# A fused attention and two-MLP kernel: its opening stage in a hand-written order

## The chip, the cores and the metric

One Trainium2 chip, of which the kernel uses one core. The metric is device time in microseconds for one execution; lower is better. Three runs of the kernel before took 1207.8, 1211.51 and 1207.32 us.

## The reference

The inputs are q, k, v (8 batches, 8 heads, 576 rows, 64 columns) and phi (the same with 32 columns), all float32; the weights W1 (512 x 2048) and W2 (2048 x 512) of the first MLP, and those of the second one, are float64 in memory.

```python
a = exp(phi - max(phi, axis=2)); a = a / (sum(a, axis=2) + 1e-9)
k_m = einsum('bhsm,bhsd->bhmd', a, k); v_m = einsum('bhsm,bhsd->bhmd', a, v)
attn = softmax(0.125 * q @ k_m.T)
x = attn @ v_m                                   # heads side by side: 8 x 576 x 512
xn = (x - mean(x)) / sqrt(var(x) + 1e-6) * g_ln
x = x + relu(xn @ W1) @ W2                       # first MLP
h = gelu(x @ w_in); u, v = halves of h           # second MLP
x = x + (u * (w_sg @ norm(v) + b_sg)) @ w_out
```

## The kernel before

The program has two phases. Phase 1 computes attention and the first MLP for the eight batches in turn, phase 2 the second MLP. All matrix products are made in float32 by splitting an operand into a high and a low part (suffixes h and l) that TensorE multiplies in separate passes.

In phase 1 attention is not multiplied out. For each batch `prep_max`, `prep_exp`, `prep_sum`, `prep_kv` and `prep_norm` make the 32 memory rows per head (`kvn`) from phi, k and v; `prep_T` turns them (`kvT`); `prep_vb` lays the value part out as `VBh`/`VBl`. For each group of query tiles (128 rows each, with a short tile of 64 at the end of a batch) `t_q` turns the tile through TensorE (`ptq`, copied to `qT`), `t_scores` makes the scores (`sc`), turns them on VectorE (`z`) and takes the exponential, `t_norm` divides by the sum, `t_attn` turns back and splits into `aTh` and `aTl`. `t_x` multiplies with VB to get x itself (`px`).

W1 is treated in four column blocks of 512 (fb = 0 to 3), each made of four row blocks (j = 0 to 3) of 128 x 512. `load_w1` brings the float64 words (`raw`), 512 KB for each row block in two loads. `to_f32` makes float32 of them: a ScalarE pass over the high words (L112), a VectorE pass over the low words (L113, one input), and a VectorE pass that joins both (L114, two inputs). `scale_w1` multiplies with the gain g1c on ScalarE, to `wc` (L498). `center_w1` subtracts the mean over rows: four matmuls with a constant column (`cm`, L504) add up the row blocks and spread the mean, VectorE subtracts (L506). `make_vw` multiplies the centered block with the memory's value part (`pvw`, L544), so that the hidden layer of the MLP follows directly from the attention weights, and `evict_vw` splits the result (`vw`, L550 on ScalarE, L551 on VectorE). `m1` multiplies `aT` with `vw` to the hidden tile `ph` (L592), `relu` evicts it (`hh` on ScalarE L578, `hl` on VectorE L579; `cr` is the part carried to the next batch), `m2` multiplies with W2 to `py` (L622 to L624). W2 comes in 16 chunks of 128 rows: `load_w2`, then `split_w2` with the same conversion, a cast on ScalarE (`whl`, L126) and a remainder on POOL (L127).

Batch 0 goes through the column blocks with both of its row groups (256 and 320 rows) inside, so each column block has 4 x 2 hidden tiles and needs four chunks of W2.

What sets the order: every step is put on a list with a time by `at_time`, the list is sorted, and `run_until` traces the steps. Then a scheduler orders the instructions of each engine by its own timeline; it may move what was traced later ahead of what was traced earlier. Loads are all issued by the SP queue through `load`, at most eight outstanding. `issue_after` holds an instruction behind another one.

The opening, up to time -0.4 on the list, makes batch 0's memory rows, all five query tiles of its attention (two groups of two and the short one), the first W1 block, and the first chunks of W2. Of the calls that place W1's blocks:

```python
at_time((-26.5, -26.2, -2.5, 2.0)[fb], load_w1, fb)
at_time((-16.5, -5.0, 3.0, 7.5)[fb], scale_w1, fb)
at_time((-16.4, -0.3, 4.6, 9.1)[fb], center_w1, fb)
```

Of the kernel before, what the change touches and what calls it, by code (L numbers as in the profile page):

```python
# [9 lines left out]
F32 = mybir.dt.float32  # L10
# [5 lines left out]
ALU = mybir.AluOpType  # L16
# [8 lines left out]
ORDER = mybir.DependencyInfo(mybir.DependencyClass.Sync, mybir.DependencyReason.DATA)  # L25


@with_exitstack
def fused_kernel(ctx: ExitStack, tc: tile.TileContext, q, k, v, phi, g1, w1, w2, w_in, g2, w_sg, b_sg, w_out, out):
    nc = tc.nc  # L30
    PE, V, A, G = nc.tensor, nc.vector, nc.scalar, nc.gpsimd

    B, H, S, D = q.shape
    NM = phi.shape[3]
    DM = H * D
    FF = w1.shape[1]
    P = 128
    NF = FF // P
    NFB = FF // DM
    KC = DM // P  # L40
# [26 lines left out]
    mean = mcol.to_broadcast([P, P])  # L67
    mhalf = const.tile([P, 3], F32, name="mhalf")
    G.memset(mhalf, -0.5)
    g1c = const.tile([P, KC], F32, name="g1c")  # L70
    g2c = const.tile([P, KC], F32, name="g2c")
# [10 lines left out]
        return t[:, 0, :], t[:, 1, :]  # L82

    def load(out_ap, in_ap):
        return nc.sync.dma_start(out=out_ap, in_=in_ap)  # L85

    def rsqrt_of(tmp, x, on_v):

# [54 lines left out]
    def phase1():  # L143
# [24 lines left out]
        def ps_of(b, shape, name):  # L168
            return ps_0(shape, name) if b == 0 else ps_a.tile(shape, F32, tag="a", name=name)
# [307 lines left out]
        W2, WC, VW, raws = {}, {}, {}, {}  # L477

        def wc_tiles():
            return [tail.tile([P, 2, DM], F32, tag="wc", name="wc", bufs=4) for _ in range(2)]  # L480

        def load_w1(fb):

            raws[fb] = []
            for j in range(KC):
                t = wpool.tile([P, DM], I64, tag="w", name="raw1")
                for g in range(2):
                    r0 = g * 4 * D + j * D
                    load(t[64 * g:64 * g + 64, :], w1[r0:r0 + D, fb * DM:(fb + 1) * DM])
                raws[fb].append(t)  # L490

        def scale_w1(fb):

            WC[fb] = ws = wc_tiles()
            for j, raw in enumerate(raws.pop(fb)):
                d = ws[j // 2][:, j % 2, :]
                w = to_f32(raw, [st.get("hl", tiles[TB - 1]["tr"])] if fb else None)
                A.activation(d, w, AF.Copy, scale=g1c[:, j:j + 1])  # L498

        def center_w1(fb):  # L500
            ws = WC[fb]
            cm = ps_of(fb, [P, DM], "cm")
# [131 lines left out]
        def at_time(time, fn, *a):  # L634
            ev.append((time, seq[0], fn, a))
            seq[0] += 1
# [9 lines left out]
        for b in range(B):  # L646
            pair, odd = divmod(b, 2)
# [10 lines left out]
            for n, gs in enumerate([[0], [1]] if b == 0 else [[0, 1]]):  # L658
                at_time(pb - (4.3 if b == 3 else 5) * f, load_phi, b, gs)
                at_time(pb + 0.2 * n, prep_max, b, gs)  # L660
                at_time(pb + 0.1 + 0.2 * n if b == 0 else pb + f, prep_exp, b, gs)
            at_time(pb + (1.6 if b else 6) * f, prep_sum, b)
            kv_at = (4.0, 6.7) if b == 0 else (5.2, 7.4) if odd and b > 1 else (4.4, 8.4)
            at_time(pb - 2 if b == 0 else pb + 0.6 * f, load_rem, b)
            if b > 1:
                at_time(pb + 7.0 * f, prep_kv, b, [0, 1])
            for g in range(2):
                if b <= 1:
                    at_time(pb + kv_at[g] * f, prep_kv, b, [g])
                for part in range(2):  # L670
                    n = 2 * g + part
                    if b == 0:
                        kv_from = pb - 4 + n
                    elif b == 1:
                        kv_from = pb + (0.5 * part if g == 0 else kv_at[0] + 0.1 + 0.01 * part) * f
                    else:
                        kv_from = pb + (0.5 + 1.2 * n) * f
                    at_time(kv_from, load_kv, b, g, part)
            if b == 0:
                for g in range(2):  # L680
                    at_time(pb + 9.3 * f, prep_norm, b, g)
            at_time(first - 0.6, prep_T, b)
            at_time(first + (0.8 if b == 1 else 3), prep_vb, b)
# [50 lines left out]
        def run_until(time):  # L734
            while ev and ev[0][0] <= time:
                _, _, fn, a = ev.pop(0)
                fn(*a)

        for fb in range(NFB):
            at_time((-26.5, -26.2, -2.5, 2.0)[fb], load_w1, fb)  # L740
            at_time((-16.5, -5.0, 3.0, 7.5)[fb], scale_w1, fb)
            at_time((-16.4, -0.3, 4.6, 9.1)[fb], center_w1, fb)
            at_time((-15, 1.3, 5.8, 10.3)[fb], make_vw, 0, [fb])
            at_time((-15, 1.3, 5.8, 10.3)[fb], evict_vw, 0, fb)
            at_time((1.4, 3.0, 7.4, 12.0)[fb], store_w1, fb)
        for c in range(NF):
            split_at = 4.5 * (c // 4) + 0.5625 * (c % 4) - 0.6 if c > 3 else 0.9 * c - 4
            at_time(split_at - 5 if c > 3 else -12.7 if c == 3 else 0.2 * c - 26.4, load_w2, c)
# [21 lines left out]
        for n in range(len(steps) + LAG):  # L770
# [4 lines left out]
            if n >= LAG:  # L775
                _, j, c = steps[n - LAG]
# [310 lines left out]
        es_left.close()  # L1087
        es_right.close()

    for g in range(2):  # L1090
        load(g1c[64 * g:64 * g + 64, :], g1[g * 4 * D:(g + 1) * 4 * D].rearrange("(c p) -> p c", p=D))
    load(g2c, g2.rearrange("(c p) -> p c", p=P))
    phase1()
    phase2()

# [29 lines left out]
```

## Time and profile before

| | |
|---|---|
| median of 3 runs | 1207.8 us (1207.32 to 1211.51) |
| span of the profiled execution | 1206.0 us, from its first to its last instruction; no separate time of that execution is given, the runs' median is 1.8 us above its span |
| TensorE matmuls busy | 1167.4 us, 97% |
| VectorE, ScalarE, POOL busy | 689.7, 467.1, 400.7 us |
| granted TensorE clock, mean | 0.990 |
| moved by DMA | 124.15 MB, mean 103 GB/s |

How to read it: busy time is the time in which an engine executes instructions; matmuls are pipelined, so their durations overlap and the distance of two starts is their price. The granted clock is 1.00 at 2.4 GHz and 0.50 at 1.2 GHz. In a timeline a row may stand for several instructions (x4); its second number is then the time from the first one's start to the last one's end. The bracket at a row's end is the idle time of the engine before it and what ended that. In a row of the DMA queue (SPq) the time is that of issuing, not of the transfer.

### The profile page before, as it was taken

What the parts mean: (1) busy time and instruction counts of PE and PEld (TensorE: products, weight loads), DVE (VectorE), ACT (ScalarE), POOL (GpSimd) and SP (SyncE); (2) the same over time, 40 slices, a digit from 0 to 9 for tenths busy, and PEclk for the clock granted to TensorE, in tenths of its full rate; (3) what the DMA queues carried; (4) which work ended last, traced back from release to release, by engine and by line L of the source; (5) the groups of instructions that cost most, each with busy time, mean ns of one, the idle gap of its engine ahead of it and who ended that gap; (6) DMA issues with size and microseconds to landing.
All of it is one profiled execution on the core that took longest, in us unless ns stands there. A gap on an engine that the chain in (4) does not pass through costs nothing.

```text
span 1206.0 us, 20725 instructions
## 1 busy us (share of the span) xinstructions
PE 1167.4 (97%) x7711; PEld 991.3 (82%) x7711; DVE 689.7 (57%) x1669; ACT 467.1 (39%) x1071; POOL 400.7 (33%) x622
## 2 busy tenths in 40 slices
PE   4699999999999999999999999999999999999998
PEld 2377678888788888788888888889989988998997
DVE  2887665755645545644645445568576477447532
ACT  3575333332432322332323445445444354344430
POOL 2133212211201211201211112456666475566641
PEclk9699999999999999999999999999999999999999
DMA  8996744373341443331410343122240042022201
GB/s 205 284 287 177 219 106 125 79 205 66 109 117 31 129 137 66 97 107 23 128 36 27 106 118 115 35 82 88 77 143 18 19 142 77 1 81 86 79 18 70
DMA packets 199141, 124.15 MB, mean 103 GB/s; under 512 B 93312, under 2 KB 174336, under 8 KB 199040
## 3 DMA queue, kind: packets, MB, share of 16 engines
q1 hardware_dynamic: 199040, 122.82, 36.4%
q8 instruction: 61, 1.00, 0.3%
q14 instruction: 40, 0.33, 0.1%
HBM read 99.72 MB, written 31.33 MB: 109 GB/s over the span
## 4 chain that ended last, share of the span: by engine, by line
PE 86%; DVE 5%; DMA 4%; SPq 2%; issue 1%; POOL 1%; ACT 1%; POOLq 0%; DVEq 0%
PE ph L592 16%; PE py L622 10%; PE py L624 10%; PE py L623 10%; PE pvs L1027 8%; PE po L1050 8%; PE pv L918 8%; PE pu L1002 7%; PE pvw L544 2%; DMA raw<-in_moe_w_ch_dram 2%; SPq L85 2%; PE kvp L315 1%; DMA q<-q_d 1%; PE cm L504 1%; PE sc L401 1%
## 5 line engine op out<-in xcount | busy, mean ns | idle before, releaser
L592 PE MATMUL ph<-aTh,vw 128*128 128x320 f32 (+1 forms) x1024 | 247.2, 300 | 3.5 <-ACT aTh L440 1.4
L622 PE MATMUL py<-whl,hh 128*128 128x512 f32 x512 | 201.8, 396 | 3.0 <-ACT hh L578 3.0
L592 PEld LDWEIGHTS ph<-aTh,vw 128*128 128x128 f32 x1024 | 178.2, 190 | 28.3 <-issue 9.4
L623 PE MATMUL py<-whl,hh 128*128 128x512 f32 x512 | 201.3, 393 | 0.0
L624 PE MATMUL py<-whl,hl 128*128 128x512 f32 x512 | 183.2, 397 | 0.0
L578 ACT ACTIVATE hh<-ph 128x256 fp32r<-128x256 f32 x256 | 96.6, 385 | 167.7 <-PE ph L592 111.5
L579 DVE SCALAR_TENSOR_TENSOR hl<-ph,hh 128x256 fp32r<-128x256 f32 x256 | 106.5, 421 | 87.6 <-ACT hh L578 87.0
L592 PE MATMUL ph<-aTl,vw 128*128 128x256 f32 (+1 forms) x512 | 152.2, 297 | 0.0
L1027 PE MATMUL pvs<-wsh,vhl 128*128 128x288 f32 x576 | 121.0, 295 | 0.0
L622 PEld LDWEIGHTS py<-whl,hh 128*128 128x128 f32 x512 | 96.3, 188 | 26.9 <-ACT hh L578 5.7
L623 PEld LDWEIGHTS py<-whl,hh 128*128 128x128 f32 x512 | 96.5, 189 | 19.3 <-issue 0.8
L1002 PE MATMUL pu<-yTh,whl 128*128 128x288 f32 x512 | 111.0, 296 | 0.3 <-DVE ug L907 0.3
L592 PEld LDWEIGHTS ph<-aTl,vw 128*128 128x128 f32 x512 | 97.1, 190 | 10.3 <-issue 2.9
L624 PEld LDWEIGHTS py<-whl,hl 128*128 128x128 f32 x512 | 89.9, 189 | 12.0 <-issue 2.3
L1027 PEld LDWEIGHTS pvs<-wsh,vhl 128*128 128x128 f32 x576 | 94.4, 188 | 0.6
L918 PE MATMUL pv<-whl,yTh 128*128 128x512 f32 x288 | 91.0, 396 | 0.0
L1050 PE MATMUL po<-whl,gh 128*128 128x512 f32 x288 | 90.0, 391 | 0.0
L1002 PEld LDWEIGHTS pu<-yTh,whl 128*128 128x128 f32 x512 | 85.4, 189 | 1.8 <-DVE ug L907 0.8
L578 ACT ACTIVATE cr<-ph 128x64 fp32r<-128x64 f32 x128 | 28.6, 226 | 130.7 <-PE ph L592 130.1
L1030 POOL TENSOR_TENSOR gt<-gt,ug 128x288 f32<-128x288 f32 x64 | 52.8, 826 | 68.5 <-DVE gt L1029 62.1
L1027 PE MATMUL pvs<-wsl,vhl 128*128 128x288 f32 x256 | 75.6, 295 | 0.0
L1002 PE MATMUL pu<-yTl,whl 128*128 128x288 f32 x256 | 75.5, 295 | 0.0
(154 smaller groups left out, 2162.4 us busy)
## 6 DMA issues: line engine op xcount, KB each, us to landing
wc<-w_d SPq DMA_DIRECT2D x28, 512.0 KB, 6.0
y_d<-x SPq DMA_DIRECT2D x36, 256.0 KB, 2.3
yt<-y_d SPq DMA_DIRECT2D x36, 256.0 KB, 2.7
yr<-y_d SPq DMA_DIRECT2D x36, 256.0 KB, 2.8
kv<-in_k_dram SPq DMA_DIRECT2D x32, 256.0 KB, 3.6
kv<-in_v_dram SPq DMA_DIRECT2D x32, 256.0 KB, 4.0
raw<-in_moe_w_ch_dram SPq DMA_DIRECT2D x32, 256.0 KB, 8.5
raw<-in_moe_w_ch_dram SPq DMA_DIRECT2D x16, 512.0 KB, 6.1
```

The lines of the kernel that those rows point to most:

```text
L85: return nc.sync.dma_start(out=out_ap, in_=in_ap)
L578: high = A.activation(out_h, src, AF.Relu)
L579: return high, V.scalar_tensor_tensor(out=out_l, in0=src, scalar=0.0, in1=out_h.bitcast(F32), op0=ALU.max, op1=ALU.subtract)
L592: R["ph"] = PE.matmul(ph, w_[:, ks], x[:, g, 0:w], start=(n == 0), stop=(n == 3 * HK - 1))
L622: PE.matmul(py, hh, wh, start=start, stop=False)
L623: PE.matmul(py, hh, wl, start=False, stop=False)
L624: PE.matmul(py, hl, wh, start=False, stop=stop)
L918: PE.matmul(pv, y[:, kc, cs], w, start=(n == 0), stop=(n == 3 * KC - 1))
L1002: PE.matmul(pu, w[:, ds_], y[:, kc, cs], start=(n == 0), stop=(n == 3 * KC - 1))
L1027: PE.matmul(pvs, v_, w_, start=(n == 0), stop=(n == len(ops) - 1))
L1030: G.tensor_tensor(out=gt, in0=gt, in1=ug, op=ALU.mult)
L1050: PE.matmul(po, gg[:, dc, cs], w, start=(n == 0), stop=(n == 3 * KC - 1))
```

## The change

Three things. A wrapper `Traced` stands around the engines and SP; while a switch is on, each instruction that goes through it is kept in the order in which it was traced on its engine. The switch is on for everything up to time -0.4 on the list and off behind it. Second, the times of the opening are new: phi first, then k and v, then the gains (which came first), query tiles 0 and 1, W1's first block, query tiles 2 and 3 and the short one, W2's chunks 0 to 3, W1's second block. `scale_w1` is called for one row block at a time, between the steps of the softmax. Third, `center_w1` uses one matmul on a sum of the four row blocks; `sum_w1` makes that sum by three additions, on POOL, but for the last one of the first block, which is on VectorE.

```diff
+class Traced:
...
+        return lambda *args, **kw: self._tc.keep_in_program_order(f(*args, **kw))
...
-    PE, V, A, G = nc.tensor, nc.vector, nc.scalar, nc.gpsimd
+    pinned = {"on": False}
+    PE, V, A, G, SP = (Traced(tc, e, pinned) for e in (nc.tensor, nc.vector, nc.scalar, nc.gpsimd, nc.sync))
...
-        def scale_w1(fb):
-
-            WC[fb] = ws = wc_tiles()
-            for j, raw in enumerate(raws.pop(fb)):
+        def scale_w1(fb, js=range(KC)):
+
+            if js[0] == 0:
+                WC[fb] = wc_tiles()
+            ws = WC[fb]
+            for j in js:
+                raw = raws[fb][j]
...
+        def sum_w1(fb, j):
+            ws = WC[fb]
+            total = raws[fb][0].bitcast(F32)[:, 0:DM]
+            E = G if fb or j < KC - 1 else V
+            E.tensor_tensor(out=total, in0=ws[0][:, 0, :] if j == 1 else total, in1=ws[j // 2][:, j % 2, :], op=ALU.add)
...
             cm = ps_of(fb, [P, DM], "cm")
-            for j in range(KC):
-                PE.matmul(cm, mean, ws[j // 2][:, j % 2, :], start=(j == 0), stop=(j == KC - 1))
+            PE.matmul(cm, mean, total, start=True, stop=True)
...
+                    at_time(-60 + 0.1 * g, load_phi, b, [g])
...
+                at_time(-58.5, load_gains)
...
-                        at_time(-27, load_q, us[i], ub, qi)
-                        at_time(-21 + 0.1 * tt, t_q, gr, i)
+                        at_time((-58, -56, -55.9)[gi], load_q, us[i], ub, qi)
+                        at_time((-45.5, -40, -39)[gi], t_q, gr, i)
...
-                    at_time(-17 + 0.1 * tt, t_scores, gr)
-                    at_time(-16 + 0.1 * tt, t_norm, gr)
-                    at_time(-16 + 0.1 * tt, t_attn, gr)
+                    at_time((-43, -39.5, -38.9)[gi], t_scores, gr)
+                    at_time((-42, -39.35, -38.8)[gi], t_norm, gr)
+                    at_time((-41, -39.1, -38.7)[gi], t_attn, gr)
...
+            at_time((-42.5, -41.5, -40.5, -39.6)[j], scale_w1, 0, [j])
...
-            at_time((-26.5, -26.2, -2.5, 2.0)[fb], load_w1, fb)
...
+            at_time((-57, -30, -2.5, 2.0)[fb], load_w1, fb)
...
+        pinned["on"] = True
         run_until(-0.4)
+        pinned["on"] = False
```

Where it moves instructions. First ScalarE, before, at the end of W1's first block (its row blocks are `raw_222` to `raw_231`, behind all copies of query tiles). `raw_236` to `raw_245` are the row blocks of W1's second block, `raw` without a number is a chunk of W2, `z` the softmax groups (two of 512 columns, and a short one of 128).

```order
L112 ACTIVATE raw_228<-raw_228 128x512
L498 ACTIVATE wc<-raw_225,g1c 128x512
L112 ACTIVATE raw_231<-raw_231 128x512
L498 ACTIVATE wc<-raw_228,g1c 128x512
L498 ACTIVATE wc<-raw_231,g1c 128x512
L112 ACTIVATE raw<-raw 128x512
L112 ACTIVATE raw_236<-raw_236 128x512
L112 ACTIVATE raw_239<-raw_239 128x512
L415 ACTIVATE z_358<-z_358 128x512
L112 ACTIVATE raw_242<-raw_242 128x512
L415 ACTIVATE z_375<-z_375 128x512
```

The same engine in the changed kernel, from W1's third row block on (L36 is the wrapper's line, which each kept instruction carries; `raw_184` to `raw_193` are W1's first block, `qT_353` query tiles 2 and 3, `qT_418` the short tile).

```order
L36 ACTIVATE raw_190<-raw_190 128x512
L36 ACTIVATE wc<-raw_190,g1c 128x512
L36 COPY qT_353<-ptq 128x4x128 x2
L36 ACTIVATE raw_193<-raw_193 128x512
L36 ACTIVATE wc<-raw_193,g1c 128x512
L36 ACTIVATE z_381<-z_381 128x512
L36 CAST vw<-pvw 128x512 x2
L36 CAST aTh<-z_381 128x2x256
L36 COPY qT_418<-ptq 128x256
L607 ACTIVATE hh<-ph 128x256 x3
```

The copies of query tiles 2 and 3 now stand between the third and the fourth row block of W1, the short tile behind the first `vw`, and no pass over W1's second block (L112 of `raw_236` and on) stands ahead of the first hidden tiles any more.

Next POOL in the changed kernel, behind the sum of phi: `raw_184` is the first W1 block's sum, `raw_466` the second's, `VBl` the low part of V, `whl` the remainders of W2.

```order
L36 TENSOR_TENSOR raw_184<-wc 128x512
L36 TENSOR_TENSOR aTl<-z_320,aTh 128x2x256
L36 TENSOR_TENSOR raw_184<-raw_184,wc 128x512
L36 TENSOR_TENSOR VBl_145<-kvn,VBh_144 32x2x64 x4
L36 TENSOR_TENSOR whl<-raw,whl 128x512 x3
L524 TENSOR_TENSOR raw_466<-wc 128x512
L524 TENSOR_TENSOR raw_466<-raw_466,wc 128x512
L36 TENSOR_TENSOR whl<-raw,whl 128x512
L524 TENSOR_TENSOR raw_466<-raw_466,wc 128x512
L139 TENSOR_TENSOR whl<-raw,whl 128x512
```

Before, there stood only `VBl`, `aTl` and five remainders in a row; now `VBl` is behind the first block's sum, and three additions stand among the remainders.

Last VectorE in the changed kernel, up to the second W1 block's mean (`wc<-wc,cm`) and its `vw`; `raw_496` and `raw_499` belong to W1's third block.

```order
L126 SCALAR_TENSOR_TENSOR raw_496<-raw_496 128x512
L125 TENSOR_SCALAR raw_499<-raw_499 128x512
L608 SCALAR_TENSOR_TENSOR hl<-ph,hh 128x256
L126 SCALAR_TENSOR_TENSOR raw_499<-raw_499 128x512
L125 TENSOR_SCALAR raw<-raw 128x512
L126 SCALAR_TENSOR_TENSOR raw<-raw 128x512
L535 TENSOR_TENSOR wc<-wc,cm 128x1024 x2
L125 TENSOR_SCALAR raw<-raw 128x512
L564 MEMSET pvw 128x2
L478 BN_STATS s_711<-x 128x6
L564 MEMSET pvw 128x2
```

Before, that subtraction stood ahead of the third block's passes; now all four of the third block and one of W2 stand ahead of it.

## Rows read from the trace of the kernel before

**Rows 1.** The page: busy time of the engines, and the chain by engine.
```profile
PE 1167.4 (97%) x7711; PEld 991.3 (82%) x7711; DVE 689.7 (57%) x1669; ACT 467.1 (39%) x1071; POOL 400.7 (33%) x622
PE 86%; DVE 5%; DMA 4%; SPq 2%; issue 1%; POOL 1%; ACT 1%; POOLq 0%; DVEq 0%
```

**Rows 2.** Stretches: length, PE, PEld, DVE, ACT, POOL busy, clock, DMA share, GB/s.
```profile
40.00:60.00 20.00, 14.03 (x57) 7.68 (x56) 18.87 (x43) 12.14 (x23) 3.08 (x3) 0.71 1.03 303
80.00:90.00 10.00, 10.00 (x50) 7.57 (x50) 8.91 (x18) 4.59 (x10) 4.67 (x8) 1.00 0.76 173
```

**Rows 3.** Stretches of 2 us in which the clock changes level.
```profile
26.00:28.00 2.00, 0.00 (x0) 0.00 (x0) 1.12 (x2) 0.90 (x2) 0.00 (x0) 0.89 1.00 231
54.00:56.00 2.00, 1.09 (x4) 0.37 (x2) 2.00 (x6) 0.86 (x2) 0.00 (x0) 0.78 1.00 242
```

**Rows 4.** Timeline of SP's queue: start, us, what it issues.
```profile
0.72 1.44 SPq L85 DMA_DIRECT2D g1c<-in_moe_g_ln_dram  x2
3.96 1.26 SPq L85 DMA_DIRECT2D prz<-in_phi_dram  x2
...
12.62 7.47 SPq L85 DMA_DIRECT2D q<-in_q_dram  x10
20.13 36.12 SPq L85 DMA_DIRECT2D raw<-in_moe_w_ch_dram  x32
```

**Rows 5.** Timeline of TensorE in the opening: start, us, what, [idle before].
```profile
19.05 2.30 PE L376 MATMUL ptq<-ident,q 128*128 128x128 f32 x12
...
35.42 6.55 PE L504 MATMUL cm<-wc,mcol 128*128 128x512 f32 x8
45.81 3.06 PE L544 MATMUL pvw<-wc,kvT 64*32 64x512 f32 x16 [3.85 <-DVE wc L506]
49.82 0.58 PE L592 MATMUL ph<-aTh,vw 128*128 128x256 f32 x1 [0.95 <-ACT vw L550]
```

**Rows 6.** Timeline of ScalarE in the opening.
```profile
32.84 0.69 ACT L112 ACTIVATE raw<-raw 128x512 f32<-128x512 f32 x1 [0.97 <-DMA raw<-in_moe_w_ch_dram]
33.43 1.61 ACT L498 ACTIVATE wc<-raw,g1c 128x512 f32<-128x512 f32 x2
...
37.04 0.67 ACT L112 ACTIVATE raw<-raw 128x512 f32<-128x512 f32 x1 [1.35 <-DMA raw<-in_moe_w_ch_dram]
...
43.52 0.67 ACT L112 ACTIVATE raw<-raw 128x512 f32<-128x512 f32 x1 [1.05 <-DMA raw<-in_moe_w_ch_dram]
```

**Rows 7.** Timeline of VectorE: the mean's subtraction, and conversion passes in a row.
```profile
44.54 2.35 DVE L506 TENSOR_TENSOR wc<-wc,cm 128x1024 f32<-128x1024 f32 x2
...
67.16 1.42 DVE L113 TENSOR_SCALAR raw<-raw 128x512 uint32<-128x512 uint32 x4
68.51 2.49 DVE L114 SCALAR_TENSOR_TENSOR raw<-raw 128x512 uint32<-128x512 uint32 x4
```

**Rows 8.** Timeline of POOL: prz's memset, the low parts of V, one remainder.
```profile
3.13 0.31 POOL L159 MEMSET prz<- 128x256 f32 x1
...
22.83 2.02 POOL L346 TENSOR_TENSOR VBl<-kvn,VBh 32x128 fp32r<-32x128 f32 x4 [6.66 <-ACT VBh L343]
...
78.90 1.31 POOL L127 TENSOR_TENSOR whl<-raw,whl 128x512 fp32r<-128x512 f32 x1
```

**Rows 9.** Timeline of VectorE beside that remainder.
```profile
79.15 1.34 DVE L113 TENSOR_SCALAR raw<-raw 128x512 uint32<-128x512 uint32 x1
```

**Rows 10.** Timeline of TensorE at W1's second block and third mean.
```profile
75.89 0.28 PE L592 MATMUL ph<-aTh,vw 128*128 128x256 f32 x1
...
77.55 0.40 PE L623 MATMUL py<-whl,hh 128*128 128x512 f32 x1
77.78 0.39 PE L624 MATMUL py<-whl,hl 128*128 128x512 f32 x1
...
79.38 3.60 PE L504 MATMUL cm<-wc,mcol 128*128 128x512 f32 x8
```

**Rows 11.** Timeline of TensorE in batch 1's preparation.
```profile
148.40 0.50 PE L622 MATMUL py<-whl,hh 128*128 128x512 f32 x1 [1.98 <-ACT hh L578]
```

More of the change, by code (lines that the diff above doesn't have):

```diff
@@ L25, with __init__, __getattr__ @@
 ORDER = mybir.DependencyInfo(mybir.DependencyClass.Sync, mybir.DependencyReason.DATA)
+class Traced:
+    def __init__(self, tc, engine, pinned):
+        self._tc, self._engine, self._pinned = tc, engine, pinned
+    def __getattr__(self, name):
+        f = getattr(self._engine, name)
+        if not self._pinned["on"]:
+            return f
+        return lambda *args, **kw: self._tc.keep_in_program_order(f(*args, **kw))
 @with_exitstack
@@ L84, in load @@
     def load(out_ap, in_ap):
-        return nc.sync.dma_start(out=out_ap, in_=in_ap)
+        return SP.dma_start(out=out_ap, in_=in_ap)
     def rsqrt_of(tmp, x, on_v):
@@ L480, in wc_tiles, with load_gains @@
             return [tail.tile([P, 2, DM], F32, tag="wc", name="wc", bufs=4) for _ in range(2)]
+        def load_gains():
+            for g in range(2):
+                load(g1c[64 * g:64 * g + 64, :], g1[g * 4 * D:(g + 1) * 4 * D].rearrange("(c p) -> p c", p=D))
+            load(g2c, g2.rearrange("(c p) -> p c", p=P))
         def load_w1(fb):
@@ L498, in scale_w1 @@
                 A.activation(d, w, AF.Copy, scale=g1c[:, j:j + 1])
+        def sum_w1(fb, j):
[3 more added lines that the diff above has]
+            E.tensor_tensor(out=total, in0=ws[0][:, 0, :] if j == 1 else total, in1=ws[j // 2][:, j % 2, :], op=ALU.add)
         def center_w1(fb):
             ws = WC[fb]
+            if fb:
+                for j in range(1, KC):
+                    sum_w1(fb, j)
+            total = raws.pop(fb)[0].bitcast(F32)[:, 0:DM]
             cm = ps_of(fb, [P, DM], "cm")
-            for j in range(KC):
-                PE.matmul(cm, mean, ws[j // 2][:, j % 2, :], start=(j == 0), stop=(j == KC - 1))
+            PE.matmul(cm, mean, total, start=True, stop=True)
             for n in range(2):
@@ L657, in phase1 @@
             pb = first - 11 * f
[L658 to L678, printed above, removed]
@@ L679, in phase1 @@
             if b == 0:
                 for g in range(2):
-                    at_time(pb + 9.3 * f, prep_norm, b, g)
-            at_time(first - 0.6, prep_T, b)
-            at_time(first + (0.8 if b == 1 else 3), prep_vb, b)
+                    at_time(-60 + 0.1 * g, load_phi, b, [g])
+                    at_time(-50 + 0.2 * g, prep_max, b, [g])
+                    at_time(-49.9 + 0.2 * g, prep_exp, b, [g])
+                    for part in range(2):
+                        at_time(-59 + 0.3 * g + 0.1 * part, load_kv, b, g, part)
@@ new lines, in phase1 @@
+                    at_time(-48 + 1.5 * g, prep_kv, b, [g])
+                    at_time(-45, prep_norm, b, g)
+                at_time(-58.8, load_rem, b)
+                at_time(-58.5, load_gains)
+                at_time(-46, prep_sum, b)
+                at_time(-44.5, prep_T, b)
+                at_time(-38, prep_vb, b)
+            else:
+                at_time(pb - (4.3 if b == 3 else 5) * f, load_phi, b, [0, 1])
+                at_time(pb, prep_max, b, [0, 1])
+                at_time(pb + f, prep_exp, b, [0, 1])
+                at_time(pb + 1.6 * f, prep_sum, b)
+                kv_at = (5.2, 7.4) if odd and b > 1 else (4.4, 8.4)
+                at_time(pb + 0.6 * f, load_rem, b)
+                if b > 1:
+                    at_time(pb + 7.0 * f, prep_kv, b, [0, 1])
+                for g in range(2):
+                    if b == 1:
+                        at_time(pb + kv_at[g] * f, prep_kv, b, [g])
+                    for part in range(2):
+                        n = 2 * g + part
+                        if b == 1:
+                            kv_from = pb + (0.5 * part if g == 0 else kv_at[0] + 0.1 + 0.01 * part) * f
+                        else:
+                            kv_from = pb + (0.5 + 1.2 * n) * f
+                        at_time(kv_from, load_kv, b, g, part)
+                at_time(first - 0.6, prep_T, b)
+                at_time(first + (0.8 if b == 1 else 3), prep_vb, b)
@@ L737, in run_until @@
                 fn(*a)
+        for j in range(KC):
+            at_time((-42.5, -41.5, -40.5, -39.6)[j], scale_w1, 0, [j])
+            if j:
+                at_time((None, -41.4, -40.4, -39.55)[j], sum_w1, 0, j)
         for fb in range(NFB):
-            at_time((-26.5, -26.2, -2.5, 2.0)[fb], load_w1, fb)
[L741 to L745, printed above, removed]
+            at_time((-57, -30, -2.5, 2.0)[fb], load_w1, fb)
+            if fb:
+                at_time((None, 1.2, 3.0, 7.5)[fb], scale_w1, fb)
+            at_time((-39.4, 2.2, 4.6, 9.1)[fb], center_w1, fb)
+            at_time((-39.3, 2.8, 5.8, 10.3)[fb], make_vw, 0, [fb])
+            at_time((-39.3, 2.8, 5.8, 10.3)[fb], evict_vw, 0, fb)
+            at_time((1.4, 4.0, 7.4, 12.0)[fb], store_w1, fb)
         for c in range(NF):
             split_at = 4.5 * (c // 4) + 0.5625 * (c % 4) - 0.6 if c > 3 else 0.9 * c - 4
-            at_time(split_at - 5 if c > 3 else -12.7 if c == 3 else 0.2 * c - 26.4, load_w2, c)
+            at_time(split_at - 5 if c > 3 else 0.2 * c - 35, load_w2, c)
             at_time(split_at, split_w2, c)
         ev.sort(key=lambda e: (e[0], e[1]))
+        pinned["on"] = True
         run_until(-0.4)
+        pinned["on"] = False
         QUARTERS = [[*range(4 * fb, 4 * fb + 4)] for fb in range(NFB)]
@@ L1088, in phase2 @@
         es_right.close()
-    for g in range(2):
-        load(g1c[64 * g:64 * g + 64, :], g1[g * 4 * D:(g + 1) * 4 * D].rearrange("(c p) -> p c", p=D))
-    load(g2c, g2.rearrange("(c p) -> p c", p=P))
     phase1()
```

## The prediction

> **What bounds the kernel now.** I read the page first: TensorE is busy 97% of the span and holds 86% of the chain that ended last [rows 1], so behind the opening every microsecond that TensorE is spared is a candidate for the total. Then the stretches: from 40 to 60 us TensorE is busy 14.03 of 20 us at a mean granted clock of 0.71; from 80 to 90 us it is busy all the time at 1.00, and VectorE is at 8.91 of 10 [rows 2]. So there are two stages with different limits: an opening in which TensorE waits for data and for VectorE, and behind it a stage in which TensorE is full and VectorE nearly so. The granted clock leaves full speed (2.4 GHz) between 26 and 28 us, after TensorE had run out of work, and is back only between 54 and 56 us [rows 3], some 5 us after the first `ph` matmul at 49.82 [rows 5].
>
> How the opening ends: SP issues the gains, phi, k and v, then all ten q loads (7.47 us), and only then W1, from 20.13 [rows 4]. ScalarE takes up W1's fourth block at 32.84, and the last `wc` is written at 33.43 + 1.61 = 35.04 [rows 6]. The four mean matmuls (`cm`) take 6.55 us from 35.42, at half clock [rows 5]; VectorE, busy with softmax, subtracts the mean only from 44.54 [rows 7], 2.6 us after `cm` has ended. `pvw` ends at 45.81 + 3.06 = 48.87, and the first `ph` starts at 49.82 [rows 5]. Meanwhile ScalarE has made its first pass over the four blocks of W1's second column block, from 37.04 to 43.52 [rows 6]: work done in idle time.
>
> **The change, part by part.** My sums are against the profiled execution (span 1206.0 us). The median run is 1207.8; I take the 1.8 us between them as a constant.
>
> *SP.* The three gain loads (two take 1.44, so three some 2.1 [rows 4]) leave the front. That does not start k and v earlier: prz's load now stands second, and it has to wait for POOL's memset of prz, which ends at 3.44 [rows 8]; before, its issue came at 3.96 [rows 4] and lost nothing by that wait. So k and v go out as before, and the gains' 2.1 us follow them. Six of the ten q issues go behind W1: 6 x 0.75 = 4.5 us. Net, W1 is issued 2.4 us earlier, and its fourth block is there at 32.8 - 2.4 = 30.4. The second pair of q tiles now lands behind W1: four issues at the old 0.75, so at about 33.4.
>
> *The path to the first `ph`.* ScalarE's order puts the two copies of that second pair (`qT_353`) ahead of W1's fourth block, so the block that is there at 30.4 lies until q is there: 33.4, plus the second tile's four transposes at half clock (12 took 2.30 at full clock [rows 5], so 4 x 2 x 0.19 = 1.5), plus a copy, 0.6: 35.5. Then ScalarE's pass over the block, 0.69 [rows 6], VectorE's, 0.62 [rows 7], the scaling, 0.8: 37.7. The last addition of the row sum is on VectorE, 0.62, as for another instruction with two such operands [rows 7]: 38.4. One `cm` in place of four: 6.55 / 4 = 1.64: 40.1. VectorE's second softmax batch is about through by then, so the subtraction starts at 40.5 where it started at 44.54. The rest is as before: `ph` starts at **45.8, a gain of 4.0**; between 2.5 and 5.5 if q lands 1.5 us later or earlier.
>
> *Behind it the gain is paid back.* The third, short query tile and all conversions of W2 and of W1's second block now stand behind this point. TensorE has 24 matmuls of 256 columns (0.23 apart at half clock, as 512 columns at full clock [rows 10]: 5.5 us) and then needs the short tile's softmax: at about 54.2, an estimate for its chain of short operations. Only then VectorE begins on W2. What it must do, by its order, before it subtracts the second block's mean: 14 first passes at 1.42 / 4 and 13 second passes at 2.49 / 4 [rows 7], 13.1 us, and eight short evictions and a normalization, about 3.5: 70.8. Then the subtraction, 2.35 [rows 7], one more pass and the two memsets that `pvw` waits for, 1.2, `pvw` at full clock, 1.0, and the eviction, 0.95 [rows 5]: 76.3. That is the lower bound for the second block's first `ph`, which came at 75.89 [rows 10].
>
> The upper bound comes from POOL. In that stretch it now has the low parts of V (2.02), four remainders of W2 and the three new additions, at 1.31 each [rows 8]: 11.2 us. The rows show what happens when the two engines meet: VectorE's first pass, 0.355 in a row of four [rows 7], took 1.34 when it began at 79.15 [rows 9], beside a POOL instruction that ran from 78.90 to 80.21 [rows 8]: it lasted until POOL was done. If all of POOL's time but 3.5 us under short evictions is added to VectorE's, the first `ph` comes at 76.3 + 7.7 = 84.0. I take the middle, 80.2, **+4.3** against 75.89: the collision at 79.15 speaks for the upper end, VectorE's evictions and waits, under which POOL runs free, for the lower.
>
> The Trainium skill, "SBUF — State Buffer", section "Who interferes with whom", says that a VectorE instruction in a two-port mode, or with two SBUF inputs against a GpSimd one that reads SBUF, contends with GpSimd, and that the one that comes second is blocked for the whole instruction. By that rule additions on an idle GpSimd are not free, which speaks against this change; the pass at 79.15 agrees (1.34 against 0.355), and the sum by it is the upper bound.
>
> At that `ph` TensorE has done more than before: nine `py` matmuls at 0.23 (2.1) that came later, less a pair of `px` (0.7) still to do. And it has less to come: three of the four `cm` of W1's third and fourth block. Four took 3.60 at full clock, with some overlap at the ends [rows 10], so three are some 2.6 each time. Up to the third block: 4.3 - 1.4 - 2.6 = +0.3. The fourth: -2.6. The six additions of these two blocks (6 x 1.31) meet a VectorE that is nearly full at 80 to 90 us [rows 2]: between nothing and 3.9, those of one block; I take 0.9, since they fall in 20 us and not in a few.
>
> *Sum:* +0.3 - 2.6 + 0.9 = **-1.4 us**. With the lower bound throughout it is 0.4 - 1.4 - 2.6 - 2.6 = -6.2, with the upper one 8.1 - 1.4 - 2.6 - 2.6 + 3.9 = +5.4. From about 130 us on all engines have the order of before, so what stands there stays. 1207.8 - 1.4 = **1206.4**.
>
> **The rivals.**
> *Faster.* POOL and VectorE rarely meet, and the 5.2 us of `cm` come through in full: -6.2. q lands early, and VectorE begins on W2 1.5 us earlier: -7.7. TensorE waits 1.98 us at 148 us for an eviction held up by the next batch's softmax [rows 11]; if that chain gains as much as TensorE, half of it goes: -8.7, so 1199.1. For it: VectorE has gaps to lose before 54 us. Against it: the 16.6 us counted on VectorE leave none after.
>
> *Slower.* VectorE and POOL alternate throughout (+5.4), and TensorE, which waits for the short tile at 52 and again before the second block, is put back to 1.2 GHz, as between 26 and 28 us after it had run out of work [rows 3]. One more rise like that from 49.82 to about 55 [rows 3, 5] costs half of 5 us: 2.5. Together +7.9: 1215.7. It decides if the second block's first `ph` comes later than 84 us.
>
> *Nothing moves in the opening.* The second q pair holds W1's fourth block so long that "W1 ahead of later query tiles" does not do what it says: `ph` starts at 48, and what follows is 2.2 us later: +0.8, 1208.6.
>
> **How the numbers follow.** Forecast (the payment about eats the gain) 0.55, faster rival 0.18, slower rival 0.15, nothing in the opening 0.12. About 0.5%, 6 us, is what a measurement of this kernel can tell from no change (its three runs spread over 4.2). The forecast's own bounds, 1201.6 and 1213.2, and the third rival lie within it but for their edges: within 0.5% 0.68, faster by more 0.17, slower by more 0.15. For 8 in 10 the range takes in the faster rival and goes up to the near side of the slower one: 1199 to 1214.
>
> **What would show it.** In the new profile: the first `ph` near 45.8, and ScalarE idle before W1's fourth block, waiting for `qT`'s transposes; a wait of TensorE of 2 us or more near 52; the second block's first `ph` between 78 and 83, with VectorE full before it and its passes stretched to a microsecond beside POOL's additions; `cm` as a single matmul. The forecast is wrong if that `ph` comes at 76 or earlier (then faster), if the clock falls again after 50 us (slower), or if TensorE shows a wait after 130 us that the old trace does not have.

## The result, and the profile after

The changed kernel takes 1219.3 us (median of 4 runs, 1217.95 to 1220.3) where the kernel before takes 1208.6 beside it: a ratio of 1.0087, 95% interval 1.0071 to 1.0104. It is **slower by 0.9%**, 10.7 us, outside the predicted range of 1199 to 1214. The profiled execution has a span of 1216.8 us against 1206.0.

The page, to be held against [rows 1]: TensorE has 3.9 us less to do, VectorE 11.9 and GpSimd 15.8 us more, and of TensorE's groups one that did not wait before (0.0), the `py` matmuls with the low half (`hl`), now waits 4.4 us for VectorE (last column: idle time ahead of the group, and who ended it).

```profile
PE 1163.5 (96%) x7687; PEld 988.6 (81%) x7687; DVE 701.6 (58%) x1670; ACT 467.1 (38%) x1071; POOL 416.5 (34%) x633
PE 85%; DVE 6%; DMA 3%; issue 2%; POOL 1%; ACT 1%; SPq 1%; POOLq 0%; DVEq 0%
L653 PE MATMUL py<-whl,hl 128*128 128x512 f32 x512 | 183.8, 400 | 4.4 <-DVE hl L608 4.4
```

Rows picked from TensorE's timeline of the changed kernel, which answer to [rows 5, 10, 11]:

```profile
30.92 2.11 PE L36 MATMUL ptq<-ident,q 128*128 128x128 f32 x8 [9.26 <-DMA q<-in_q_dram]
36.69 2.04 PE L36 MATMUL cm<-raw,mcol 128*128 128x512 f32 x2 [1.87 <-DVE raw L36]
40.05 3.06 PE L36 MATMUL pvw<-wc,kvT 64*32 64x512 f32 x16 [1.31 <-DVE wc L36]
43.82 0.39 PE L621 MATMUL ph<-aTh,vw 128*128 128x256 f32 x1
51.39 0.56 PE L621 MATMUL ph<-aTh,vw 128*128 128x320 f32 x2 [2.22 <-ACT aTh L36]
71.86 1.22 PE L653 MATMUL py<-whl,hl 128*128 128x512 f32 x2 [3.71 <-DVE hl L608]
76.30 1.76 PE L533 MATMUL cm<-raw,mcol 128*128 128x512 f32 x2
81.61 1.96 PE L573 MATMUL pvw<-wc,kvT 64*32 64x512 f32 x16 [2.37 <-DVE pvw L564]
84.29 0.58 PE L621 MATMUL ph<-aTh,vw 128*128 128x256 f32 x1 [0.71 <-ACT vw L579]
112.11 1.22 PE L282 MATMUL mb<-dg,mcol 128*128 128x256 f32 x2 [2.20 <-DVE vw L580]
158.38 0.50 PE L651 MATMUL py<-whl,hh 128*128 128x512 f32 x1 [3.16 <-ACT hh L607]
```

The first `ph` starts 6.0 us earlier (43.82 against 49.82 [rows 5]), the second block's first `ph` 8.4 us later (84.29 against 75.89 [rows 10]). So 14.4 us are lost between these two. Then the offset stays: the fourth block's `pvw` starts 8.8 us late (135.84 against 127.05), batch 1's third `pvw` 10.0 us late (168.05 against 158.08), the last 1048 us add 0.8.

The granted clock of the changed kernel in stretches of 2 and 4 us (columns as in [rows 2]):

```profile
72.00:76.00 4.00, 4.00 (x10) 3.13 (x11) 3.78 (x8) 2.10 (x4) 0.00 (x0) 0.50 0.99 265
78.00:80.00 2.00, 1.24 (x9) 0.80 (x7) 1.90 (x2) 1.19 (x3) 0.00 (x0) 1.00 0.43 123
84.00:88.00 4.00, 3.71 (x17) 3.71 (x18) 1.58 (x3) 4.00 (x8) 4.00 (x6) 0.50 1.00 308
88.00:90.00 2.00, 1.41 (x6) 0.73 (x5) 1.91 (x5) 1.48 (x4) 1.53 (x2) 0.99 1.13 293
112.00:114.00 2.00, 1.89 (x7) 1.71 (x8) 1.28 (x3) 0.20 (x1) 1.30 (x1) 0.50 0.00 0
160.00:162.00 2.00, 2.00 (x8) 1.84 (x8) 1.25 (x4) 0.40 (x2) 0.00 (x0) 0.50 0.70 138
```

Around the waits at 68, 80, 110 and 156 us the clock falls to 1.2 GHz, where before it stayed full from 56 us on. TensorE is busy for 11.6 us in the four half-speed stretches shown. About half of that (an estimate) would have done at 2.4 GHz, since the `py` matmuls start 0.43 us apart there (72.88, 73.31, 73.74) and 0.23 apart at full clock [rows 10].

Why TensorE waits at 71.86: VectorE (rows picked), and beside it GpSimd, in the changed kernel.

```profile
51.58 0.42 DVE L36 TENSOR_SCALAR raw<-raw 128x512 uint32<-128x512 uint32 x1
53.23 0.69 DVE L36 SCALAR_TENSOR_TENSOR raw<-raw 128x512 uint32<-128x512 uint32 x1 [1.23 <-ACT raw L36]
...
55.24 1.38 DVE L36 SCALAR_TENSOR_TENSOR raw<-raw 128x512 uint32<-128x512 uint32 x1 [0.46 <-ACT raw L36]
...
63.41 1.79 DVE L36 SCALAR_TENSOR_TENSOR raw<-raw 128x512 uint32<-128x512 uint32 x1
65.26 1.39 DVE L125 TENSOR_SCALAR raw<-raw 128x512 uint32<-128x512 uint32 x1
66.57 1.78 DVE L126 SCALAR_TENSOR_TENSOR raw<-raw 128x512 uint32<-128x512 uint32 x1
68.27 1.52 DVE L125 TENSOR_SCALAR raw<-raw 128x512 uint32<-128x512 uint32 x1
69.71 1.76 DVE L126 SCALAR_TENSOR_TENSOR raw<-raw 128x512 uint32<-128x512 uint32 x1
71.39 0.41 DVE L608 SCALAR_TENSOR_TENSOR hl<-ph,hh 128x256 fp32r<-128x256 f32 x1
...
78.10 2.35 DVE L535 TENSOR_TENSOR wc<-wc,cm 128x1024 f32<-128x1024 f32 x2 [2.22 <-PE cm L533]
```

```profile
62.88 1.77 POOL L36 TENSOR_TENSOR whl<-raw,whl 128x512 fp32r<-128x512 f32 x1 [4.17 <-ACT whl L36]
64.61 1.75 POOL L524 TENSOR_TENSOR raw<-wc 128x512 f32<-128x512 f32 x1
66.44 1.36 POOL L524 TENSOR_TENSOR raw<-raw,wc 128x512 f32<-128x512 f32 x1
67.77 1.74 POOL L36 TENSOR_TENSOR whl<-raw,whl 128x512 fp32r<-128x512 f32 x1
69.47 1.45 POOL L524 TENSOR_TENSOR raw<-raw,wc 128x512 f32<-128x512 f32 x1
```

The five conversion passes from 63.41 on take 1.79, 1.39, 1.78, 1.52 and 1.76, 8.2 us together; alone, as at 51.58 and 53.23, they are two of 0.42 and three of 0.69, 2.9. Each ends 0.3 to 0.6 us after a GpSimd instruction has ended (64.65, 66.36, 67.80, 69.51, 70.92), that is, after a little less time than the pass itself needs: it ran when GpSimd was done. That holds for the passes with one input (`TENSOR_SCALAR`, 1.39 and 1.52) as for those with two. Three of those five are W1's additions (L524), two are W2's remainders. The `hl` that TensorE waits for stands behind the passes.

### The profile page after: what moved, and what is told of

It reads as the page before. It is cut to its first block, busy times and chain, and to the rows that moved or that the text cites. A ratio compares the mean times of both kernels' runs of the same rounds, so it can differ in the third digit from the quotient of the medians.

```text
span 1216.8 us, 20703 instructions
## 1 busy us (share of the span) xinstructions
PE 1163.5 (96%) x7687; PEld 988.6 (81%) x7687; DVE 701.6 (58%) x1670; ACT 467.1 (38%) x1071; POOL 416.5 (34%) x633
## 4 chain that ended last, share of the span: by engine, by line
PE 85%; DVE 6%; DMA 3%; issue 2%; POOL 1%; ACT 1%; SPq 1%; POOLq 0%; DVEq 0%
PE ph L621 16%; PE py L651 10%; PE py L653 10%; PE py L652 10%; PE pvs L1072 8%; PE po L1095 8%; PE pv L963 8%; PE pu L1047 7%; PE pvw L573 2%; PE kvp L327 1%; DMA q<-q_d 1%; SPq L36 1%; DVE raw L125 1%; DVE qT L391 1%; PE sc L413 1%
## 5 line engine op out<-in xcount | busy, mean ns | idle before, releaser
L436 POOL TENSOR_TENSOR z<-z,r 128x512 f32<-128x512 f32 (+2 forms) x18 | 16.9, 941 | 172.5 <-DVE r L435 119.1
```

## The experiments

Two theories. **A**: the additions on GpSimd hold VectorE up. **B**: the written order costs by itself, because ScalarE and VectorE may no longer take up what is ready. Medians are of 4 to 10 runs; percentages are against runs of the kernel before on the same chip, brackets are 95% intervals of the difference. A "point" below is one such per cent, 12 us. No experiment leaves work out.

**1. The sums of the later blocks taken back** (`sum_first_only`):

```
-            if fb:
-                for j in range(1, KC):
-                    sum_w1(fb, j)
...
-            PE.matmul(cm, mean, total, start=True, stop=True)
+            if fb:
+                for j in range(KC):
+                    PE.matmul(cm, mean, ws[j // 2][:, j % 2, :], start=(j == 0), stop=(j == KC - 1))
+            else:
+                PE.matmul(cm, mean, total, start=True, stop=True)
```

> The changed kernel with its hand-written opening, but the mean of W1's second to fourth column block again from four cm matmuls; the row-block sum stays for the first block. Theory A (GpSimd's nine additions stretch VectorE's conversion passes): the five passes that took 8.24 us between 63.4 and 71.5 us shrink by 4 us or more, the wait of 3.71 us for hl goes or falls below 1 us, and the 7.9 us of cm matmuls that come back are about paid for: 1215 to 1219 us. Theory B (the conversions come too late because the written order holds them behind the opening; the additions hardly matter): TensorE pays the nine matmuls (9 x 0.88 = 7.9 us) without a return, 1224 to 1227 us.

1214.6 us, +0.49% [0.29, 0.68]: 0.38 points better than the change although TensorE does nine matmuls more. As A says, the 3.71 us wait is gone and the five passes take 4.2 us less; but the second block's `pvw` still starts only at 78.27, and 6 us of loss are left that A does not explain:

```profile
78.27 1.40 PE L574 MATMUL pvw<-wc,kvT 64*32 64x512 f32 x16 [1.96 <-DVE pvw L565]
```

**2. The kernel before with the sums** (`before_with_sums`):

```
...
+            for j in range(1, KC):
+                E = G if fb or j < KC - 1 else V
+                E.tensor_tensor(out=total, in0=ws[0][:, 0, :] if j == 1 else total, in1=ws[j // 2][:, j % 2, :], op=ALU.add)
...
-            for j in range(KC):
-                PE.matmul(cm, mean, ws[j // 2][:, j % 2, :], start=(j == 0), stop=(j == KC - 1))
+            PE.matmul(cm, mean, total, start=True, stop=True)
```

> The kernel before, its order left to the scheduler, with only the mean changed: row blocks summed, one cm matmul for each of the four column blocks. Theory A (additions on GpSimd collide with VectorE): the gain of the matmuls (4.9 us at half clock for the first block, 7.9 us for the others) is eaten by VectorE, 1206 to 1212 us. Theory B (the order is at fault): TensorE keeps most of it, 1197 to 1203 us, and the first ph starts some 4 us earlier.

1212.8 us, +0.31% [0.19, 0.43]: 0.8 us above A's range and far from B's. Not as forecast by either: the first `ph` comes at 49.38, hardly earlier than before, though the first block's `pvw` starts at 39.44 and no longer at 45.81 [rows 5]: TensorE then stands for 6.88 us, until ScalarE has the high part of the softmax (`aTh`). And the second block's `pvw` starts at 78.89, not at 67.19.

**3. The change with no written order** (`order_left_free`):

```
-        pinned["on"] = True
```

> The changed kernel with nothing kept in written order: its new times and its sums stay, the scheduler places each engine's instructions. Theory A: as slow as the change, 1216 to 1221 us, since the same additions meet the same conversions. Theory B: ScalarE and VectorE again convert W1's second block and W2 in the gaps of the opening, the clock does not fall again after 60 us, 1200 to 1208 us.

1209.0 us, +0.04% [-0.10, 0.18]. With the same sums and the same times, 10 us of the 10.7 are gone: B, though 1 us above its range. The clock part of B's forecast was wrong: it falls here too (0.75 on average from 70 to 80 us), round two waits at the second block:

```profile
72.92 1.09 PE L573 MATMUL pvw<-wc,kvT 64*32 64x512 f32 x16 [3.14 <-DVE pvw L564]
76.97 0.58 PE L621 MATMUL ph<-aTh,vw 128*128 128x256 f32 x1 [2.95 <-ACT vw L579]
```

**4. The kernel before with the first block's sum alone** (`before_sum_first`; the edit of 2, with the four `cm` kept under `if fb`):

> The kernel before with the row-block sum for the first column block only; no addition on GpSimd falls behind the opening, and nothing is kept in written order. Theory A and B both: the first ph some 4 us earlier (three cm matmuls at half clock, 4.9 us, less one addition of 0.7 us), and with it 1203 to 1206 us; if an earlier start only runs into the same conversions of W2 and W1's second block, nothing is gained, 1207 to 1209 us.

1209.0 us, +0.02% [-0.08, 0.13]. The first `ph` comes 2.5 us earlier (47.34, after a wait of 6.28 us for `aTh`) and nothing of it reaches the end: at batch 1's third `pvw` 1.1 us are left, and the span is the same. Against this version, `before_with_sums` has only the later blocks' additions more: they cost 3.7 us in the scheduler's order too, and move the second block's `pvw` from 64.40 to 78.89.

**5. The additions on VectorE** (`sums_on_vector`):

```
-            E = G if fb or j < KC - 1 else V
+            E = G if fb == 0 and j < KC - 1 else V
```

> The changed kernel, order and sums as they are, but the nine additions for W1's second to fourth column block on VectorE instead of GpSimd. If it is GpSimd's additions that stretch VectorE's passes (an addition holds VectorE up for as long as it lasts, 1.3 us and more), VectorE gives 0.62 to 0.69 us for each instead and the stretched passes of 63.4 to 71.5 us go back to 0.4 and 0.7: 1211 to 1215 us, below the version with the cm matmuls back (1214.6). If VectorE is simply short of time there, whoever adds, the additions on it make it worse: 1219 to 1224 us.

1214.9 us, +0.58% [0.37, 0.80]. Given nine more additions, the engine that is short of time is done earlier. So it is the collision and not the amount of work (A). What it costs is known only roughly: 3.5 us, give or take 3.3 by the two intervals. The passes go back to 0.41 and 0.68 but where they meet W2's remainder. It does not beat the version with the matmuls.

**6 to 8. A free order with the first sum alone, and parts of the written order.** `free_sum_first` is 1 and 3 together. `order_until_first_vw` lets go after the first block's eviction:

```
+        run_until(-38.05)
+        pinned["on"] = False
         run_until(-0.4)
-        pinned["on"] = False
```

`three_queues_kept` leaves VectorE and ScalarE unwrapped:

```
+    PE, G, SP = (Traced(tc, e, pinned) for e in (nc.tensor, nc.gpsimd, nc.sync))
+    V, A = nc.vector, nc.scalar
```

> The changed kernel's times with nothing kept in written order, and the row-block sum for the first column block only. The two faults apart and both gone: against the free order with all sums (1209.0 us) the additions behind the opening fall away and nine cm matmuls (7.9 us) come back. If the collisions cost more than the matmuls in a free order too: 1203 to 1207 us. If the additions hurt only where the written order bunches the conversions: 1211 to 1216 us.

> The changed kernel, all sums, but the written order is kept only up to the eviction of the first block's vw; the short query tile and all conversions of W2 and of W1's second block are left to the scheduler. If what costs is that these stand in a written order behind the short tile, most of the 10 us between the change (1219.3) and its free order (1209.0) comes back: 1209 to 1213 us, the first ph still near 44 us and the second block's near 78 us. If the first part of the written order costs it (ScalarE and VectorE wait in it for q tiles and W1 rows while other work is ready): 1216 to 1220 us.

> The changed kernel, all sums, with the written order kept on TensorE, GpSimd and SP only; VectorE and ScalarE are left to the scheduler. If the written order hurts because VectorE and ScalarE may not fill their gaps with conversions: 1208 to 1213 us. If it hurts through the loads (W1's second block and W2 issued behind six q loads) or through TensorE's order: 1216 to 1220 us.

1211.4 us, +0.21% [0.07, 0.34]; 1216.7, +0.67% [0.46, 0.88]; 1214.7, +0.55% [0.37, 0.73]. In `free_sum_first` the second forecast held: in this free order, taking the later additions out won nothing. The other two lie between the change (+0.87%) and its free order (+0.04%). Kept up to the first `vw`, the order still has 0.63 of these 0.83 points, as the second forecast had it: what costs is mostly the part before the first hidden tiles. Kept on TensorE, GpSimd and SP alone, it still has 0.51 points, 1214.7 us, between the two forecasts: by these figures (uncertain by some 0.25) ScalarE and VectorE, which B names, are not the greater part.

**9. W1's second block ahead of W2 again** (`second_block_first`, with the time of W2's fourth load also as before):

```
-                at_time((None, 1.2, 3.0, 7.5)[fb], scale_w1, fb)
-            at_time((-39.4, 2.2, 4.6, 9.1)[fb], center_w1, fb)
+                at_time((None, -5.0, 3.0, 7.5)[fb], scale_w1, fb)
+            at_time((-39.4, -0.3, 4.6, 9.1)[fb], center_w1, fb)
...
```

> The changed kernel, hand-written order and all sums, but with the kernel before's times for W1's second column block: its conversion, mean and subtraction stand ahead of W2's first four chunks again, instead of behind them. If pvw of the second block, 81.6 us in the change and 67.2 before, is late because VectorE has eight W2 passes to do first: it starts at 70 to 76 us, 1210 to 1215 us. If TensorE only changes what it waits for (W2's first chunk, which it needs for py, now comes last): a wait of 5 us and more for whl before 70 us, 1216 to 1221 us.

1219.9 us, +0.88% [0.56, 1.20]. `pvw` does start at 73.06, as the first forecast has it, and it is worth nothing: TensorE's queue now stands for 11.5 us before the one `cm`, which must wait until GpSimd has made the whole sum (and not, as forecast, for `whl`). Four `cm` matmuls can start with the first row block: in version 14, where W1's second block is also loaded earlier, the first of them starts at 56.17 after a wait of 1.35 us.

```profile
65.58 2.08 PE L533 MATMUL cm<-raw,mcol 128*128 128x512 f32 x2 [11.53 <-POOL raw L524]
```

**10 and 11. The same in a free order**, with W1's second block also loaded ahead of W2, all sums in one, the first block's alone in the other (the edits of 3 and 9, in the second that of 1 too, and):

```
-            at_time((-57, -30, -2.5, 2.0)[fb], load_w1, fb)
+            at_time((-57, -36, -2.5, 2.0)[fb], load_w1, fb)
```

> The same with nothing kept in written order, and with the loads of W1's second block ahead of W2's as well. Against the free order of the changed times (1209.0 us, pvw of the second block at 72.9 us): if that pvw sets the total, 1204 to 1207 us with pvw at 68 to 71 us; if the late W2 chunks take its place, 1208 to 1213 us.

> The same as free_second_block_first, with the row-block sum for the first column block only, so nine cm matmuls (7.9 us) for six to nine additions on GpSimd. If additions are harmless where the order is free, it is slower than that version by some 2 us, as 1211.4 stood to 1209.0; if they hurt where conversions are bunched, it is faster by 2 to 4 us.

1213.5 us, +0.39% [0.27, 0.51], with `pvw` at 65.49, just outside both forecasts, and **1203.9 us, -0.40% [-0.56, -0.24]**: the fastest version here, 4.8 us below the kernel before. Here the additions of the later blocks make 9.6 us, in a free order too: with all sums `cm` waits 2.77 us at 57.74 for GpSimd's sum, and the third block's `pvw` comes at 105.67 instead of 88.79. So the additions do hurt here, and by more than the 2 to 4 us of the forecast. Without them TensorE has no gap from 60 to 100 us worth naming (columns as in [rows 2]):

```profile
60.00:80.00 20.00, 20.00 (x117) 15.46 (x116) 18.74 (x37) 16.00 (x33) 10.27 (x11) 1.00 1.05 332
80.00:100.00 20.00, 19.81 (x119) 16.09 (x117) 19.65 (x41) 12.22 (x28) 5.61 (x10) 1.00 0.79 223
```

**12 and 13. The new times without any sum**, in a free and in the written order (the edit of 1 without its `if`, and no `sum_w1`); **14 and 15**: version 11 in the written order, and without its sum.

> The new times and loads alone: no written order and no sums, four cm matmuls for each of the four column blocks as before. Against the kernel before it shows what W1's load ahead of six q loads is worth. By theory B: first ph 2 to 4 us earlier than 49.8 us, but W1's second block behind W2 and its pvw at 68 to 72 us, 1207 to 1212 us. If the load order itself is the gain that the rest spoils: 1202 to 1206 us.

> The change without its sums: hand-written order and new times, four cm matmuls for each column block. The same without the written order took 1206.5 us. If the written order costs by itself (conversions of W2 and of W1's second block only behind the short query tile): 1212 to 1217 us, pvw of the second block at 76 to 80 us. If it costs only together with the additions: 1206 to 1209 us.

> The fastest version so far (1203.9 us, free order, W1's second block loaded and converted ahead of W2, row-block sum for the first block only) with its opening kept in the written order. If the written order costs by itself: 1210 to 1215 us, the clock low again behind 60 us. If its cost was the additions' and the second block's late conversion, both gone here: 1204 to 1207 us.

> The fastest version so far (1203.9 us) without its one row-block sum: four cm matmuls for the first block too. If the first block's sum shortens the opening: first ph 1.5 to 4 us later than 42.1 us and 1205 to 1208 us. If the opening is anyway not what sets the total: 1203 to 1205 us.

1206.5 us, -0.20% [-0.34, -0.06]; 1218.1, +0.99% [0.84, 1.14]; 1214.5, +0.62% [0.45, 0.79]; 1204.7, -0.26% [-0.38, -0.15]. Without any addition the written order costs 1.2 points, and 1.0 in the version that is otherwise the fastest; with all sums it is 0.8 (the change against 3), with the first block's sum alone only 0.3 (1 against `free_sum_first`). `kept_no_sums` is 1 us above its first forecast, `free_no_sums` has its first `ph` 10 us earlier where 2 to 4 were forecast. `kept_second_first_sum1` comes out as its first forecast has it, the clock at 0.74 from 60 to 70 us. In the last version the first `ph` came earlier (40.10), not later, so the first block's sum is not what makes version 11 fast.

What the written order does is seen between 12 and 13, whose list of work is the same. In the free order (SP's queue, then ScalarE, then TensorE):

```profile
3.99 2.09 SPq L97 DMA_DIRECT2D prz<-in_phi_dram  x2
15.58 4.99 SPq L97 DMA_DIRECT2D raw<-in_moe_w_ch_dram  x8
```

```profile
21.06 0.69 ACT L124 ACTIVATE raw<-raw 128x512 f32<-128x512 f32 x1 [1.94 <-DMA raw<-in_moe_w_ch_dram]
```

```profile
30.59 4.72 PE L531 MATMUL cm<-wc,mcol 128*128 128x512 f32 x8
39.50 0.38 PE L619 MATMUL ph<-aTh,vw 128*128 128x256 f32 x1
```

In the written order:

```profile
5.57 0.61 SPq L36 DMA_DIRECT2D kv<-in_k_dram  x1
17.38 4.99 SPq L36 DMA_DIRECT2D raw<-in_moe_w_ch_dram  x8
```

```profile
24.31 0.63 ACT L36 ACTIVATE z<-z 128x512 f32<-128x512 f32 x1 [3.07 <-DVE z L36]
24.85 0.64 ACT L36 ACTIVATE raw<-raw 128x512 f32<-128x512 f32 x1
```

```profile
30.31 2.03 PE L36 MATMUL ptq<-ident,q 128*128 128x128 f32 x8 [8.35 <-DMA q<-in_q_dram]
35.27 5.26 PE L36 MATMUL cm<-wc,mcol 128*128 128x512 f32 x6
45.58 0.39 PE L619 MATMUL ph<-aTh,vw 128*128 128x256 f32 x1 [0.30 <-ACT vw L36]
```

The last `cm` row is cut by its window at 40 us: six of the eight matmul records. SP's free order issues the first k at 1.76 and prz's loads behind the first k and v; the written one has prz's load second in its queue and issues k at 5.57, and W1 1.8 us later. The free order takes up W1's first row block when it has landed, at 21.06; the written one stands 3.07 us before a softmax step that is not ready, and takes it at 24.85. TensorE stands 8.35 us before the second q pair, with the scores and `cm` behind. The first `ph` comes 6.1 us later, the second block's `pvw` 9.0 (78.03 against 68.99), the fourth's 12.0 (136.43 against 124.47); the spans of the profiled executions differ by 11.7. How much of it each of these waits costs was not tried one by one.

**The change in four steps**, each a version that ran:

| version | against the kernel before | step |
|---|---|---|
| new times and loads, free order, four `cm` | -0.20% [-0.34, -0.06] | -2.4 us |
| the same in the written order | +0.99% [0.84, 1.14] | +14.4 us |
| with the first block's sum | +0.49% [0.29, 0.68] | -6.0 us |
| with all sums: the change | +0.87% [0.71, 1.04] | +4.6 us |

The steps are differences of the ratios times 1208 us, each uncertain by 2 to 3 us by the two intervals. Between the spans of the profiled executions (1206.0, 1203.8, 1215.5, 1213.7, 1216.8) the steps are -2.2, +11.7, -1.8 and +3.1: the same signs, and the written order the largest. (That 14.4 us also stand between the two `ph` above is chance.) They belong to this path: in a free order the scheduler places everything anew with each edit, and differences of 2 or 3 us between free versions (`free_no_sums`, `free_sum_first`, `order_left_free`) are not put down to a cause here.

## Why the prediction was wrong, point by point

- *SP.* Right about the change: k goes out at 5.57 as prz's load waits, and W1 3.1 us earlier (17.06; the forecast said 2.4 [rows 4]).
- *The path to the first `ph`.* Mechanism right, size short: 6.0 us gained, 4.0 forecast. ScalarE did hold W1's fourth block behind both copies of the second pair, but q was there at 30.9 and not 33.4:

```profile
33.07 0.58 ACT L36 COPY qT<-ptq 128x512 f32<-128x512 f32 x1 [0.18 <-PE ptq L36]
33.55 0.69 ACT L36 ACTIVATE raw<-raw 128x512 f32<-128x512 f32 x1
```

- *The short tile.* Right: TensorE waits for it before 51.39 (2.22 us).
- **The step that failed first: "I take the middle", 80.2, some 4 of the 12.2 us between forecast and span.** VectorE began on W2 at 51.58, 2.6 us before the forecast, and yet the second block's `ph` came at 84.29, past the upper bound of 84.0. From its first W2 pass to the subtraction (78.10) it took 26.5 us where I had counted 16.6 of work and up to 7.7 of collisions. The collisions came in full: the passes lost 7.4 us, the five above 5.3 of it. What I had not counted are waits inside VectorE's list, 3.9 us: 1.23 and 0.46 for ScalarE's pass of the same chunk, one chunk after the other, and 2.22 for `cm`, which stood in TensorE's queue behind `py` matmuls at 1.2 GHz. (The work itself was then 1.4 less than counted.) My lower bound let VectorE work through its list without a wait. In the written order without additions (`kept_no_sums`) it does not either: the same stretch takes 22.4 us (52.97 to 75.41) and `ph` comes at 79.84, not 76.3. So of the 26.5 us the additions make some 4.
- **The second, and the largest: "TensorE has done more, and less to come", -1.4 and -2.6 twice, some 6 us.** The count was right (48 `py` matmuls before that `ph` against 39, one pair of `px` missing), but the time was not won: from the second block's `ph` to the fourth block's `pvw` TensorE took 51.6 us, 51.2 before. The matmuls spared were given back in waits (2.20 at 112.11, 0.71, 0.66) and at half clock.
- **The third: "what stands there stays"** behind 130 us, 2.0 us. The wait of [rows 11] grew from 1.98 to 3.16 us, and the clock fell after it.
- *A reading that was wrong.* The clock of the kernel before was not low throughout from 28 to 54 us: the granted clock was 1.00 from 42 to 44 us, after the `cm` matmuls, and 0.50 again from 46 on. [rows 3] skips that. No term of the sum hangs on it.
- *The slower rival* (0.15; VectorE and GpSimd alternate, the clock falls, decided at 84 us) is what the trace shows, and its 1215.7 was 3.6 short; it had one more fall of the clock, the trace has four. But the runs give its mechanism a smaller part: the later blocks' additions are some 4.6 us of the change, of which the collision is some 3.5, both known to about 3 us. The Trainium skill, "SBUF — State Buffer", section "Who interferes with whom", has a VectorE instruction with two SBUF inputs contend with a GpSimd instruction that reads SBUF, and the second to issue blocked until the first is done; the passes of 1.79 and 1.76 us beside 1.77 and 1.45 on GpSimd agree.
- *No rival had the main cause.* I priced the moves that the list names, and took a written order as the same work at other places. That it forbids each queue to go on with what is ready costs 14.4 us in `kept_no_sums` against `free_no_sums` (11.7 by their spans). The clock is not that cause: its mean is 0.990 in both profiled executions. (The mean of 0.996 for `kept_second_first_sum1` is no measure: its trace has no clock record before 44 us, and `cm` and `pvw` take 2.04 and 3.05 us there, as they do in the change at 1.2 GHz.)

What stays open: how much of the change's loss the clock's falls make, and which of the written order's waits costs how much. A version that keeps TensorE busy in its waits was not tried, nor one that mends a single place of the order.

## What to carry to other kernels

Where a written order replaces a scheduler, cost each place at which an engine, or the queue of loads, may now stand before work that is not ready while later work is; the list of operations alone does not show it. One matmul on a finished sum is not four matmuls less: it cannot start before the last row block, and what makes the sum must be an engine that does not hold up the one that feeds it. And a gain at the first stage counts only if the stages behind it have room: 2.5 us earlier were worth nothing in `before_sum_first`.

## What was not expected of the hardware

The collision costs both sides: GpSimd's instruction of 1.31 us [rows 8] took 1.74 to 1.77 in three of the five rows beside VectorE's passes. An addition that only replaces TensorE's work can so slow two engines: in the written order nine of them cost some 4.6 us more than the nine `cm` matmuls, 0.9 us each [rows 10], that they spared. It is no rule: in a free order they cost 3.7 us in the kernel before and 9.6 in the fastest version, and nothing between `order_left_free` and `free_sum_first`.
